# Clustered attention and feed-forward: one-hot rows by a wide transposition and small DMAs, a finer start, squares moved, and GpSimd held during the norm

## The chip, the cores and the metric

The kernel runs on one core of one Trainium2 chip. The metric is device microseconds (us) of the slowest core, here the only one, as the median of several executions. Before the change it took 359.23 us in three runs (358.73 to 359.6). Engines: PE is TensorE, PEld its weight loads, DVE VectorE, ACT ScalarE, POOL GpSimd, SP SyncE, which issues most of the DMAs.

## The reference

```python
# 4 batches, 8 heads, 768 tokens, head size 64, 16 clusters
q_assign = argmax(q_n @ c_n)          # cluster of each query, likewise of each key
mask     = q_assign == k_assign       # attend only inside a cluster
attn     = softmax(where(mask, q @ k.T / 8, -1e9))
x        = attn @ v                   # 3072 tokens x 512
xn       = x / sqrt(mean(x*x) + 1e-6) * rms_g
out      = (silu(xn @ w_gate) * (xn @ w_val)) @ w_out     # 512 -> 1536 -> 512
```

## The kernel before

The work is cut into eight units of half a batch (384 queries by 768 keys, eight heads each). The mask costs no operation of its own: 16 one-hot rows of the cluster stand below the 64 rows of queries and keys, and one product over 80 rows gives the scaled score plus the agreement of the clusters. For each head of a unit ScalarE takes three exponentials of 128x768; "gap n" is the place in TensorE's order ahead of the n-th of them. The first batch has no earlier work to hide its preparation in. For it, the one-hot rows are made pair by pair of heads:

```python
    pads = xp.tile([P, H // 2, 2, NB, 32], BF16, tag="gvT", name="pads")

    def pair_clusters(p, ps=None):        # products with the centroids, maximum, compare
        g, h = divmod(2 * p, HG)
        cl = cluster_products(g, [(h, 0), (h + 1, 0), (h, 1), (h + 1, 1)], ps)
        compare(pads[:, p, :, :, :NC]..., cl, largest(cl))

    def under(n, m, e0=0, e1=2):          # one head's rows, transposed straight into place
        nc.vector.transpose((kext if m else qext)[g][D:D + 32, h, e0 * UQ:e1 * UQ],
                            pads[i:i + 32, n // 2, e0:e1]...)
    def pair(p):
        pair_clusters(p)
        for n in (2 * p, 2 * p + 1):
            under(n, 1)
            under(n, 0, 0, 1)
```

The feed-forward weights come in pieces that GpSimd issues between its casts. Piece i is one DMA of 384 KB for the gate and one for the values:

```python
    def load_gv(i):
        c = slice(i * DF // 4, (i + 1) * DF // 4)
        for w, of in ((wg, moe_w_gate), (wv, moe_w_val)):
            nc.gpsimd.dma_start(out=w[:, :, c], in_=of[:, c].rearrange("(c p) f -> p c f", p=P))
```

At the end of a unit come the squares (ScalarE, `L346`), the norm on VectorE from `sm` over thirteen small steps to the normalized `xn`, and then `tx`, TensorE's transposition of `xn`, which opens the feed-forward part.

The softmax here doesn't subtract the row's maximum and nothing guards it: scores larger than these inputs give would overflow.

## Time and profile before

| what, in the profile of the kernel before | us |
|---|---|
| span | 357.5 |
| first exponential | 14.00 |
| exponential 17, the third of head 5 | 34.16 |
| half clock of TensorE | 26.7 to 30.1 |
| norm of unit 0, start of `sm` to start of `xn` | 44.13 to 48.20 |
| `tx` of unit 0 | 49.32 |
| from `tx` to the end | 308.2 |

A row of a timeline has the start, the duration, the engine, the line of the program, the operation, out<-in with the shapes, and in brackets how long the engine stood idle ahead of it and what ended that. Two rows of ScalarE set the pace of the first 50 us:

```profile
14.00 1.69 ACT L312 ACTIVATE pT<-s,off 128x768 bf16<-128x768 f32 x2 [1.33 <-PE s L308]
...
34.16 2.48 ACT L312 ACTIVATE pT<-s,off 128x768 bf16<-128x768 f32 x3 [0.23 <-PE s L308]
```

The list of DMA issues (who issued it, how often, KB of one, median us from issue to landing) has two small transfers that took long:

```profile
gcol<-in_moe_rms_g_dram SPq DMA_DIRECT2D x1, 2.0 KB, 7.6
...
hold<-inv SPq DMA_DIRECT2D x1, 3.0 KB, 5.5
```

### The profile page before, as it was taken

The page shows a single profiled execution, that of the slowest core. Times are in us where ns is not written, and L with a number is a line of the kernel's source. Part 1 is how long each engine was busy: PE and PEld are TensorE (multiplying, and loading weights), DVE is VectorE, ACT ScalarE, POOL GpSimd, SP SyncE. Part 2 cuts the span into 40 slices and gives each one's busy share as a digit, 9 for nine tenths or more (in the row PEclk, how much of TensorE's full clock was granted, in tenths as well). Part 3 has the DMA queues.
Part 4 walks back from the last instruction along what each step waited for, and adds up shares of the span by engine and source line. Part 5 has one row for each costly group of instructions (what it writes and reads, how often), then busy time and mean ns, then how long its engine had stood idle before and what let it go on. Part 6 is the DMA issues. An engine that isn't in the chain of part 4 may idle for free.

```text
span 357.5 us, 7997 instructions
## 1 busy us (share of the span) xinstructions
PE 342.4 (96%) x3031; PEld 209.2 (59%) x3031; DVE 232.7 (65%) x562; ACT 264.4 (74%) x471; POOL 113.6 (32%) x228
## 2 busy tenths in 40 slices
PE   7879889999999999999999999999999999999995
PEld 3546555655675656655576556756566656655552
DVE  4899889886367764686457864687546654675430
ACT  5787987887787878877698877978778877852431
POOL 5899431894042802444042801436000000000000
PEclk9998999999999999999999999999999999999999
DMA  8999999271153112610130001000100001001002
GB/s 275 360 171 139 271 268 296 65 227 47 59 162 106 24 59 83 191 33 16 60 119 2 19 35 59 2 6 21 59 31 0 2 32 59 3 0 62 28 2 89
DMA packets 27158, 31.62 MB, mean 88 GB/s; under 512 B 4464, under 2 KB 24176, under 8 KB 27120
## 3 DMA queue, kind: packets, MB, share of 16 engines
q1 hardware_dynamic: 17808, 24.69, 20.8%
q0 software_dynamic: 8880, 5.91, 10.1%
q8 instruction: 24, 0.39, 0.5%
q10 hardware_dynamic: 432, 0.52, 0.4%
q14 instruction: 14, 0.11, 0.1%
HBM read 28.35 MB, written 6.29 MB: 97 GB/s over the span
## 4 chain that ended last, share of the span: by engine, by line
PE 85%; ACT 7%; DVE 5%; issue 2%; DMA 1%; ACTq 0%; DVEq 0%
PE o L403 17%; PE val L381 16%; PE gate L381 16%; PE s L308 16%; PE acc L326 9%; PE tq L205 5%; ACT pT L312 4%; PE sc L235 3%; PE warm L117 2%; PE tx L368 1%; ACT xn L346 1%; DVE kext L292 1%; DVE mx L243 1%; ACT qkT L211 1%; DMA out_dram<-o_sb 1%
## 5 line engine op out<-in xcount | busy, mean ns | idle before, releaser
L312 ACT ACTIVATE pT<-s,off 128x768 bf16<-128x768 f32 x192 | 171.5, 904 | 37.8 <-PE s L308 37.1
L308 PE MATMUL s<-qext,kext 80*128 80x384 bf16 x384 | 94.6, 328 | 4.3 <-ACT pT L312 3.1
L390 DVE SCALAR_TENSOR_TENSOR th<-th,gate 128x384 f32<-128x384 f32 x84 | 46.3, 552 | 49.7 <-ACT th L389 49.3
L381 PE MATMUL val<-xnT,wv 128*128 128x384 bf16 x384 | 78.1, 326 | 0.6 <-ACT th L387 0.5
L381 PE MATMUL gate<-xnT,wg 128*128 128x384 bf16 x384 | 78.3, 325 | 0.0
L403 PE MATMUL o<-wo,gvT 128*128 128x512 bf16 x288 | 70.4, 378 | 0.4 <-ACT o_sb L414 0.3
L308 PEld LDWEIGHTS <-kext 80*128 80x128 bf16 x384 | 37.3, 99 | 37.5 <-issue 12.0
L220 POOL CAST qext<-qkT 64x384 bf16<-64x384 f32 x64 | 32.4, 510 | 83.7 <-ACT qkT L211 59.4
L389 ACT ACTIVATE th<-gate 128x384 f32<-128x384 f32 x84 | 41.0, 488 | 15.8 <-PE gate L381 15.4
L381 PEld LDWEIGHTS <-wv 128*128 128x128 bf16 x384 | 36.2, 97 | 26.5 <-issue 4.4
L394 DVE SCALAR_TENSOR_TENSOR gvT<-th,val 128x384 bf16<-128x384 f32 x84 | 46.1, 549 | 6.4 <-PE val L381 1.7
L326 PEld LDWEIGHTS <-pT 128*128 128x128 bf16 x1152 | 43.6, 97 | 11.1 <-DVE x L333 1.9
L381 PEld LDWEIGHTS <-wg 128*128 128x128 bf16 x384 | 35.9, 97 | 23.9 <-issue 2.5
L326 PE MATMUL acc<-vbf,pT 128*128 128x65 bf16 x1152 | 45.8, 193 | 2.0 <-DVE x L333 1.6
L403 PEld LDWEIGHTS <-gvT 128*128 128x128 bf16 x288 | 26.9, 97 | 26.2 <-issue 0.5
L276 POOL DMA_DIRECT2D qext<-oh x48 | 23.1, 490 | 37.2 <-DVE oh L265 37.0
L205 PE MATMUL tq<-ident_f,qk 128*128 128x128 f32 x192 | 31.0, 281 | 1.2 <-PE c_ps L179 0.8
L211 ACT ACTIVATE qkT<-tq 128x384 f32<-128x384 f32 x56 | 26.4, 498 | 2.9 <-PE tq L205 2.2
L205 PEld LDWEIGHTS tq<-ident_f,qk 128*128 128x128 f32 x192 | 23.5, 143 | 7.1 <-PE c_ps L179 1.1
L414 ACT COPY o_sb<-o 128x512 f32<-128x512 f32 x23 | 13.5, 585 | 19.1 <-PE o L403 18.6
L369 DVE TENSOR_SCALAR xnT<-tx,gcol 128x384 bf16<-128x384 bf16 x32 | 12.6, 414 | 22.4 <-PE tx L368 22.3
L276 POOL DMA_DIRECT2D kext<-oh x48 | 23.1, 488 | 1.3 <-DMA qext<-oh 1.1
(68 smaller groups left out, 261.0 us busy)
## 6 DMA issues: line engine op xcount, KB each, us to landing
qk<-in_q_dram SPq DMA_DIRECT2D x32, 192.0 KB, 4.1
vs<-in_v_dram SPq DMA_DIRECT2D x32, 192.0 KB, 4.1
out_dram<-o_sb SPq DMA_DIRECT2D x23, 256.0 KB, 2.0
qk<-in_k_dram SPq DMA_DIRECT2D x30, 192.0 KB, 4.2
wg<-in_moe_w_gate_dram POOLq DMA_DIRECT2D x4, 384.0 KB, 6.8
wv<-in_moe_w_val_dram POOLq DMA_DIRECT2D x4, 384.0 KB, 8.9
wo<-in_moe_w_out_dram POOLq DMA_DIRECT2D x3, 512.0 KB, 22.8
qext<-oh POOLq DMA_DIRECT2D x48, 12.0 KB, 1.6
```

The lines of the kernel that those rows point to most:

```text
L205: nc.tensor.transpose(ps[:, i * P:(i + 1) * P], qk[:, part, 2 * i:2 * i + 2].rearrange("p t d -> p (t d)"), ident_f)
L211: nc.scalar.activation(to, ps, ACT.Copy, scale=by)
L220: on.tensor_copy(to, of)
L276: on.dma_start(out=ext[D:D + NC, h, e * UQ:(e + 1) * UQ], in_=put[g, m][32 * h + e * NC:32 * h + (e + 1) * NC])
L308: nc.tensor.matmul(ps[:, j, :w] if nt == HT else flat[:, j * w:(j + 1) * w], lhsT=kext[g % 4][:KR, hh, kc * P:(kc + 1) * P], rhs=qext[g % ...
L312: nc.scalar.activation(pT[u, h][:, n * i:n * i + n, :w], of, ACT.Exp, bias=off, scale=scale * ZS)
L326: nc.tensor.matmul(acc[:, h % 2, t], lhsT=pT[u, h][:, kc, t * P:(t + 1) * P], rhs=vbf[g % 4][:, hh, kc % HT * 2 + kc // HT], start=kc == 0 ...
L381: nc.tensor.matmul(ps, lhsT=w[:, c, f * P:(f + 1) * P], rhs=xnT[u][:, c, :n], start=c == 0, stop=c == CC - 1)
L389: nc.scalar.activation(th, ps, ACT.Tanh, scale=0.5)
L390: nc.vector.scalar_tensor_tensor(th, th, 1.0, ps, op0=ALU.add, op1=ALU.mult)
L394: nc.vector.scalar_tensor_tensor(gvT[u][:, f, :n], gates[u], 0.5, ps, op0=ALU.mult, op1=ALU.mult)
L403: nc.tensor.matmul(outs[u], lhsT=gvT[u][:, f, t * P:(t + 1) * P], rhs=wo[:, f], start=f == 0, stop=f == FC - 1)
```

## The change

Its intent is to take work off VectorE in the first 40 us and off ScalarE at the end of unit 0, so that the first `tx` comes earlier. For head pairs 1 to 3 one wide transposition of 128x768 replaces the four (later two more) narrow ones, and four DMAs carry the rows into place. The room won on VectorE takes key casts from GpSimd and the squares of unit 0 from ScalarE. The first pair's transpositions are split, so that the first score needs less; the centroid transposition gets another buffer; and GpSimd is made to wait during the norm. Cut to its core:

```diff
-        c_ps = ps_g.tile([P, P], F32, tag="gen", name="c_ps")
+        c_ps = ps_s.tile([P, P], F32, tag="s", name="c_ps")
 ...
-    pads = xp.tile([P, H // 2, 2, NB, 32], BF16, tag="gvT", name="pads")
+    both = xp.tile([P, 5, S], BF16, tag="gvT", name="pads")
+    pads = both[:, :2]...;  rows = both[:, 2:]
 ...
     def pair(p):
         pair_clusters(p)
-        for n in (2 * p, 2 * p + 1):
-            under(n, 1)
-            under(n, 0, 0, 1)
+        nc.vector.transpose(rows[:, p - 1], pads[:, 1].rearrange("p e b c -> p (e b c)"))
+        for n in (2 * p, 2 * p + 1):
+            for m in (1, 0):
+                i = 32 * (2 * m + n % 2)
+                nc.sync.dma_start(out=(kext if m else qext)[n // HG][D:D + NC, n % HG], in_=rows[i:i + NC, p - 1])
 ...
-    under(0, 1)
+    under(0, 1, 0, 1)
     under(0, 0, 0, 1)
+    under(0, 1, 1, 2)
 ...                                     # squares of unit 0
+        if u == 0:
+            nc.vector.scalar_tensor_tensor(xn[u][:, t, c], xs[u][:, t, c], 1.0, xs[u][:, t, c], op0=ALU.mult,
+                                           op1=ALU.mult, accum_out=to)
 ...                                     # order of casts and loads
     vcast(0)
+    load_gv(0)
     vcast(1)
 ...                                     # keys of heads 4 to 7 are cast on VectorE
+        casts(dve, 4, K0, K1)
 ...                                     # GpSimd held during the norm of unit 0
-            hooks = {(1, 0, 1): lambda: rms(0)}
+            idle = const.tile([P, 1], BF16)
+            hooks = {(1, 0, 1): lambda: (rms(0), nc.gpsimd.tensor_copy(idle, xn[0][:, HT - 1, DM - 1:]))}
```

More of the change, by code (lines that the diff above doesn't have):

```diff
@@ L277, in place @@
                              in_=put[g, m][32 * h + e * NC:32 * h + (e + 1) * NC])
-    pads = xp.tile([P, H // 2, 2, NB, 32], BF16, tag="gvT", name="pads")
-    nc.gpsimd.memset(pads, 0.0)
+    both = xp.tile([P, 5, S], BF16, tag="gvT", name="pads")
+    pads = both[:, :2].rearrange("p k (e b c) -> p k e b c", e=2, c=32)
+    rows = both[:, 2:]
+    nc.gpsimd.memset(pads[:, 0, :, :, NC:], 0.0)
+    nc.gpsimd.memset(pads[:, 1, :, :, NC:], 0.0)
     def pair_clusters(p, ps=None):
@@ L286, in pair_clusters, with pair @@
         cl = cluster_products(g, [(h, 0), (h + 1, 0), (h, 1), (h + 1, 1)], ps)
-        compare(pads[:, p, :, :, :NC].rearrange("p e b c -> p b e c"), cl, largest(cl))
+        compare(pads[:, min(p, 1), :, :, :NC].rearrange("p e b c -> p b e c"), cl, largest(cl))
     def under(n, m, e0=0, e1=2):
-        g, h = divmod(n, HG)
         i = 32 * (2 * m + n % 2)
-        nc.vector.transpose((kext if m else qext)[g][D:D + 32, h, e0 * UQ:e1 * UQ],
-                            pads[i:i + 32, n // 2, e0:e1].rearrange("p e b c -> p (e b c)"))
+        nc.vector.transpose((kext if m else qext)[0][D:D + 32, n, e0 * UQ:e1 * UQ],
+                            pads[i:i + 32, 0, e0:e1].rearrange("p e b c -> p (e b c)"))
+    def pair(p):
+        pair_clusters(p)
+        nc.vector.transpose(rows[:, p - 1], pads[:, 1].rearrange("p e b c -> p (e b c)"))
[3 more added lines that the diff above has]
+                nc.sync.dma_start(out=(kext if m else qext)[n // HG][D:D + NC, n % HG], in_=rows[i:i + NC, p - 1])
     pT = {}
@@ L345, in squares @@
         c = slice(DM - 2 * D, DM) if last else slice(0, DM - 2 * D)
-        nc.scalar.activation(xn[u][:, t, c], xs[u][:, t, c], ACT.Square, accum_out=sq[u][:, int(last), t:t + 1])
+        to = sq[u][:, int(last), t:t + 1]
+        if u == 0:
+            nc.vector.scalar_tensor_tensor(xn[u][:, t, c], xs[u][:, t, c], 1.0, xs[u][:, t, c], op0=ALU.mult,
+                                           op1=ALU.mult, accum_out=to)
+        else:
+            nc.scalar.activation(xn[u][:, t, c], xs[u][:, t, c], ACT.Square, accum_out=to)
     def rms(u):
@@ L472, in tokens, with casts @@
         trans(g, h, 0, on)
-    def gp_cast(n, *what):
+    def casts(on, n, *what):
         for m, e in what:
-            cast(nc.gpsimd, n // HG, n % HG, m, (e,))
+            cast(on, n // HG, n % HG, m, (e,))
+    K0, K1, Q0, Q1 = (1, 0), (1, 1), (0, 0), (0, 1)
+    pool_, dve = nc.gpsimd, nc.vector
     trans(0, 0, 1)
@@ L484 @@
     pair_clusters(0, ps_s.tile([P, UQ], F32, tag="s", name="sc"))
-    gp_cast(0, (1, 0), (1, 1), (0, 0))
-    cast(nc.scalar, 0, 1, 1)
-    gp_cast(1, (0, 0))
+    casts(pool_, 0, K0, Q0, K1)
+    casts(pool_, 1, K0, Q0)
     load_v(0)
@@ L495 @@
     tokens(0, 2)
-    gp_cast(2, (1, 0), (1, 1), (0, 0))
-    gp_cast(0, (0, 1))
-    gp_cast(1, (0, 1))
+    casts(pool_, 2, K0, K1, Q0)
     tokens(0, 3)
-    gp_cast(3, (1, 0), (1, 1), (0, 0))
     tokens(1, 0)
+    casts(pool_, 3, K0, K1, Q0)
+    casts(nc.scalar, 1, K1)
     busy(2)
-    under(0, 1)
+    under(0, 1, 0, 1)
     under(0, 0, 0, 1)
+    under(0, 1, 1, 2)
     under(1, 1)
     under(1, 0, 0, 1)
+    casts(pool_, 0, Q1)
+    casts(pool_, 1, Q1)
     vcast(0)
+    load_gv(0)
     vcast(1)
@@ L520, in second_batch @@
             load_v(n)
-    def pair(p):
-        pair_clusters(p)
-        for n in (2 * p, 2 * p + 1):
-            under(n, 1)
-            under(n, 0, 0, 1)
     def gap1():
@@ L530, in gap1, with gap8 @@
         tokens(1, 1)
-        load_gv(0)
-        gp_cast(2, (0, 1))
-        gp_cast(3, (0, 1))
+        casts(pool_, 2, Q1)
+        casts(pool_, 3, Q1)
         vcast(2)
         vcast(3)
-        gp_cast(4, (1, 0), (1, 1), (0, 0))
-        for n in range(H, H + HG):
-            load_qk(n)
-        nc.sync.dma_start(out=gcol, in_=moe_rms_g.rearrange("(c p) -> p c", p=P), allow_slow_non_contiguous=True)
+        load_qk(H)
+        load_qk(H + 1)
     def gap5():
         pair(2)
-        gp_cast(5, (1, 0), (1, 1), (0, 0))
+        load_qk(H + 2)
+        load_qk(H + 3)
+        casts(dve, 4, K0, K1)
+        casts(pool_, 4, Q0)
+        casts(pool_, 5, Q0)
+        load_gv(1)
         vcast(4)
         vcast(5)
-        load_gv(1)
-        gp_cast(6, (1, 0), (1, 1), (0, 0))
-        gp_cast(7, (1, 0), (1, 1), (0, 0))
+    def gap8():
+        pair(3)
+        nc.sync.dma_start(out=gcol, in_=moe_rms_g.rearrange("(c p) -> p c", p=P), allow_slow_non_contiguous=True)
+        for n in (5, 6, 7):
+            casts(dve, n, K0, K1)
+        for n in (6, 7):
+            casts(pool_, n, Q0)
+        load_gv(2)
         vcast(6)
@@ L551, in gap5, with gap12 @@
         for n in (4, 5):
-            gp_cast(n, (0, 1))
-        for i in range(2, 4):
-            load_gv(i)
+            casts(pool_, n, Q1)
+        load_gv(3)
         for n in (6, 7):
-            gp_cast(n, (0, 1))
+            casts(pool_, n, Q1)
         for c in range(0, FC, 4):
             load_o(c)
+    def gap12():
+        under(0, 0, 1, 2)
+        under(1, 0, 1, 2)
+        more()
     early = [lambda h=h, m=m: trans(1, h, m) for h in (2, 3) for m in (1, 0)]
-    late = [lambda h=h, m=m: (under(h, 0, 1, 2) if m else under(h + HG, 0, 1, 2), trans(2, h, m, nc.vector))
-            for h in range(HG) for m in (1, 0)]
-    first = {1: gap1, 2: early[0], 3: early[1], 4: lambda: (early[2](), early[3]()), 5: gap5, 8: lambda: pair(3),
+    late = [lambda h=h, m=m: trans(2, h, m, nc.vector) for h in range(HG) for m in (1, 0)]
+    first = {1: gap1, 2: early[0], 3: early[1], 4: lambda: (early[2](), early[3]()), 5: gap5, 8: gap8, 12: gap12,
              14: lambda: (more(), second_batch())}
```

## The prediction

> **What bounds the kernel now.** I read the page's slices first (where is TensorE not full?), then the chain, then each engine's timeline from 5 to 52 us.
>
> ```profile
> PE   7879889999999999999999999999999999999995
> ...
> DVE  4899889886367764686457864687546654675430
> ...
> PEclk9998999999999999999999999999999999999999
> ```
>
> A digit is 8.94 us. From the seventh on TensorE is full: what comes after about 60 us can only move as a block. Anything won is won before the feed-forward part of unit 0 begins, with its first transposition `tx` at 49.32 us. Before that, VectorE is the full engine, and one slice of TensorE runs at a lower clock. Stretches of 2 us (columns: TensorE, weight loads, VectorE, ScalarE, GpSimd busy; granted clock; DMA share; GB/s):
>
> ```profile
> 24.00:26.00 2.00, 0.74 (x5) 0.20 (x2) 1.92 (x4) 1.69 (x2) 2.00 (x4) 1.00 0.26 28
> 26.00:28.00 2.00, 1.69 (x21) 1.13 (x22) 1.93 (x4) 0.00 (x0) 1.82 (x5) 0.68 0.99 149
> 28.00:30.00 2.00, 2.00 (x7) 0.87 (x6) 1.94 (x4) 1.48 (x2) 1.88 (x5) 0.50 1.31 203
> ```
>
> The timelines say what TensorE and ScalarE stood for (brackets: idle time before, and its releaser):
>
> ```profile
> 26.31 0.88 PE L326 MATMUL acc<-vbf,pT 128*128 128x65 bf16 x18 [1.56 <-DVE x L333]
> ...
> 24.86 0.57 DVE L292 STREAM_TRANSPOSE qext<-pads 32x384 bf16<-32x384 bf16 x1
> ...
> 25.69 0.56 DVE L333 TENSOR_TENSOR x<-acc,inv 128x384 f32<-128x384 f32 x1
> ...
> 28.30 0.90 ACT L312 ACTIVATE pT<-s,off 128x768 bf16<-128x768 f32 x1 [2.31 <-PE s L308]
> ```
>
> Attention output `x` of the first two heads queued behind pair 2's four one-hot transpositions; TensorE stood 1.56 us for the accumulator; its clock then fell to 0.5; ScalarE stood 2.31 us. The second limit comes at the end of unit 0, from 38 to 48 us. The chain of work there (start, duration):
>
> ```profile
> 38.56 0.50 ACT xn L346 x2
> ...
> 39.85 0.50 ACT xn L346 x2
> ...
> 41.02 0.62 ACT xn L346 x2
> ...
> 43.40 0.42 ACT xn L346 x3
> ...
> 48.45 0.48 PE s L308 x2
> ```
>
> ScalarE is full (10.00 of 10 us from 40 to 50), and the squares L346 lie in its row of exponentials. Beside it runs the norm on VectorE, almost as late:
>
> ```profile
> 44.13 0.21 DVE L353 TENSOR_TENSOR sm<-ss 128x3 f32<-128x3 f32 x1 [1.07 <-ACT xn L346]
> ...
> 44.58 0.36 DVE L124 TENSOR_SCALAR half<-ms 128x3 int32<-128x3 int32 x1
> 44.97 0.41 DVE L126 TENSOR_SCALAR yi<-half 128x3 int32<-128x3 int32 x1
> ...
> 48.20 1.28 DVE L358 TENSOR_SCALAR xn<-x,ny 128x512 bf16<-128x512 f32 x3
> ...
> 86.12 0.17 DVE L124 TENSOR_SCALAR half<-ms 128x3 int32<-128x3 int32 x1
> 86.32 0.17 DVE L126 TENSOR_SCALAR yi<-half 128x3 int32<-128x3 int32 x1
> ```
>
> The same chain from `sm` to `xn` takes 4.07 us here and 2.57 us in unit 1 (85.72 to 88.29), where GpSimd does nothing; in unit 0 GpSimd casts at that time.
>
> **What the Trainium skill says.** "SBUF — State Buffer", Who interferes with whom: VectorE and GpSimd share a port pair, held by one of them for a whole instruction; copies, casts and scalar operations in a two-port mode and operations with two SBUF inputs contend with GpSimd. The 0.17 against 0.36 to 0.41 us above agrees. "VectorE: DVE Perf Modes", The three transpose paths: the transposition works in independent 32x32 blocks; so a wide one should cost by its length only, and the trace agrees: 128x384 bf16 (L265) took 576 ns, 32x384 (L292) 570. "DMA: Bandwidth & Descriptors", Queues, rings and completion order: each ring is consumed in order, and an engine alternates between the rows that have work. The trace shows both ends: 12 KB one-hot copies land in 1.6 us when little else moves, while the 3 KB `hold` took 5.5 us amid weight loads. "TensorE: Matmul & The Clock Gate", What's actually happening: an idle window of about 3.4 us halves the clock; the half-clock stretch here lasted from about 26.6 to 30.0.
>
> **The change part by part.** I count a gap for each of unit 0's 24 exponentials (0 to 23; 0.79 us apart on ScalarE when nothing holds it).
>
> *Start.* TensorE's third transposition starts at 7.25 us; the one of the centroids ended at 6.44, and their copies on VectorE at 7.14. I take it that the buffer of `c_ps` held it; with `c_ps` elsewhere about 0.8 us falls away (the trace names only the centroid product as releaser). The first pair in halves: 0.57 instead of 0.97 us before the first score, 0.4 us. First exponential: 14.00 - 1.2 = 12.8 us.
>
> *VectorE.* Removed for pairs 1 to 3: six transpositions of 0.97 and twelve of 0.57 = 12.7 us. Added: three wide ones of 0.97 = 2.9; eight casts of keys, 0.36 each (48 such casts in the trace average 356 ns) = 2.9; squares, three of about 0.56 and three of about 0.3 = 2.6; the extra half of the first pair 0.2. Net about 4 us less, and in another order. Walking it: pair 0 takes 0.58 + 0.56 + 0.66 + 3x0.57 + 0.97 + 0.57 and gaps = 5.2 us from 8.9, so to 14.1. Pair 1 (0.6 + 0.6 + 0.65 + 0.97 = 2.8) to 16.9. Pair 2's products come after score 5, about 18.7: to 21.6, casts of head 4 to 22.4, `x` of the first heads to 23.2 (25.69 + 0.56 = 26.25 before). So the stall of 1.56 us and the clock drop at 26 us go. But then the queue gets long: pair 3, 2.8 to 26.0; six casts, 2.2 alone; two late halves for queries, 1.2; only then `x` of heads 2 and 3 (0.8): 30.2 if nobody contends. GpSimd casts at the same time; if half its 0.5 us cast is waited for at each of the eight casts, 2 us more: 32. I take 31.2. Before, that `x` ended at 32.0. TensorE needs it for head 4 in gap 16, and ScalarE can be there by about 28 to 29.5. So the old stall comes back later, smaller in effect: exponential 17 starts at about 32.8 instead of 34.16. Gain so far 1.4 us, of which part may be lost to a new clock drop.
>
> *One-hot rows by DMA.* The wide result ends at 16.9; SyncE issues one row block in about 0.4 us, key then query, and landing takes about 2 us: head 2 at about 19.8. Exponential 6 could start at 12.8 + 6x0.79 + six copies of 0.37 + 0.2 = 19.95, its score 0.5 earlier: a wait of some 0.4 us. Pair 2: from 21.6, behind the loads of heads 8 and 9 in the same ring, 24.5 to 25.5, against a wish of about 24.4. Pair 3: about 29, against 32. These waits lie before the VectorE queue of gap 16 and are hidden by it unless they exceed 2 us.
>
> *Squares.* ScalarE loses three of 0.50 and three of 0.30 (pace of instruction and accumulator read in the chain): 2.4 us of a stretch in which it is full. VectorE gets them after eight single transpositions of queries (8x0.60) have left it, so it has room. All 2.4 counted.
>
> *Norm.* 4.07 to 2.57 = 1.5 us, needed so that VectorE keeps up: with exponential 23 ending near 38.8, `x` of the last heads is done at 40.5, squares 41.3, norm 43.9, `xn` 45.2. ScalarE and TensorE reach the same point at 38.8 + 6x0.79 + four copies of 0.38 = 45.1, with `tx` just after. So both paths end about together, at 45.2 to 45.4; the norm's gain isn't added a second time.
>
> *Sum.* `tx` at 49.32 - 1.4 - 2.4 = 45.5; the walk gives 45.3. About 4 us. After it TensorE is full, but GpSimd's casts of the next batch (4x1.58 = 6.3 us) now follow the norm instead of ending before it; TensorE idled about 1.7 us between 49.8 and 66, and I let that grow by a few tenths of a us. Memory traffic is denser too. Net 3.9 us: 359.2 - 3.9 = about 355.3.
>
> **Rivals.** First, the rows come late: each one-hot copy queues among weights and token loads, and one lands after 5 us as `hold` did. Then head 2 waits about 3 us, head 4 about as long, TensorE idles and drops its clock, and some 3 us of the gain go: 358. For it: DMA share around 1.0 from 2 to 24 us. Against: before those rows SyncE's ring should be empty, because the loads of heads 8 to 11 now come behind them, and a block is only 16 packets. Second, VectorE's queue in gap 16 is worse than I think: contention makes the casts 0.8 us each, and the clock halves for 3.4 us while TensorE has score, transposition and product in each gap (0.9 us a gap at full clock before): 357. For it: VectorE 9.1 to 9.6 of 10 us all through; against: the order was presumably chosen by trying. Third, casts don't contend, exponentials run nearly at ScalarE's own pace, and `tx` comes at 42 to 43: 352 to 352.5. Fourth, the gain is real at 45 us but the part after it waits for casts, one-hot copies or weights that did not move: 357.
>
> **Range and chances.** The walk ends at 355.3; first and second rival lie 2 to 3 us above, the third 3 us below. Eight in ten: 352.4 to 357.6. Faster by over 2% means below 352.0, that is, 7.2 us; ScalarE's own minimum gives at most about 7. So 0.06. Slower by over 2% needs a wait of 11 us that nothing suggests: 0.01. Within 2%: 0.93.
>
> **What would show it.** First exponential near 12.8; exponential 6 with a wait below 1 us, its releaser a product waiting for a DMA; no clock drop at 26 us, but TensorE waiting for `x` (L333) near 29 to 31; no L346 on ScalarE in unit 0; 13 norm steps of 0.16 to 0.17; `tx` at about 45.3; the rest moved as a block. I am wrong if the row copies take over 4 us to land, if VectorE's casts average over 0.6 us, if the third transposition still starts at 7.25, or if TensorE idles over 3 us between 50 and 66 us of the old count.

## The result, and the profile after

The changed kernel took 359.62 us (four runs, 359.34 to 359.93); the kernel before, in the same rounds, 359.09 (358.73 to 359.6). The ratio is 1.0014, with an interval of 0.9996 to 1.0031: the same. The class "same" had 0.93 in the prediction, but the time lies above its range, 2.0 us over 357.6.

| us in the profile | before | after | predicted |
|---|---|---|---|
| span | 357.5 | 357.4 | |
| first exponential | 14.00 | 12.55 | 12.8 |
| landing of a one-hot block | none | 5.3 (keys), 5.5 (queries) | about 2 |
| TensorE's wait ahead of head 2 | none | 4.31 | 0.4 |
| exponential 6 | 21.18 | 24.05 | 19.95 + 0.4 |
| half clock | 26.7 to 30.1 | 23.1 to 26.5 | none at 26 |
| exponential 17 | 34.16 | 36.34 | 32.8 |
| `sm` to `xn`, start to start | 4.07 | 2.57 | 2.57 |
| `tx` | 49.32 | 49.47 | 45.3 |
| from `tx` to the end | 308.2 | 307.9 | as a block |

The page's slices first, for TensorE and its clock:

```profile
PE   8958989999999999999999999999999999999996
...
PEclk9989999999999999999999999999999999999999
```

The first two digits of TensorE rose by one each, and the third fell from 7 to 5; the lower clock is still there, now in the third slice instead of the fourth. The loss begins in that slice, 17.9 to 26.8 us. The timeline of TensorE names it:

```profile
23.21 0.80 PE L319 MATMUL s<-qext,kext 80*128 80x384 bf16 x2 [4.31 <-DMA qext<-pads]
...
34.90 0.72 PE L337 MATMUL acc<-vbf,pT 128*128 128x65 bf16 x18 [1.13 <-DVE x L344]
...
49.47 0.67 PE L384 MATMUL tx<-ident,xn 128*128 128x128 bf16 x9
```

The score of head 2 waited 4.31 us for its one-hot query rows. ScalarE shows the won start, and the hole:

```profile
12.55 1.69 ACT L323 ACTIVATE pT<-s,off 128x768 bf16<-128x768 f32 x2 [0.47 <-PE s L319]
...
24.05 0.90 ACT L323 ACTIVATE pT<-s,off 128x768 bf16<-128x768 f32 x1 [4.13 <-PE s L319]
```

In the chain of work that ended last, the transfer itself is now a link (start, duration, engine, what):

```profile
15.97 0.99 DVE pads L300
16.98 0.60 SPq L304
17.62 5.45 DMA qext<-pads
23.21 0.80 PE s L319 x2
```

VectorE was on time: the wide transposition ended at 16.96, where the prediction had 16.9. SyncE issued the four blocks at 16.98, 17.62, 18.25 and 18.89. Nothing was late before the transfers were handed over; the time went between issue and landing:

```profile
kext<-pads SPq DMA_DIRECT2D x6, 24.0 KB, 5.3
qext<-pads SPq DMA_DIRECT2D x6, 24.0 KB, 5.5
```

What did the DMA engines do then? The rows of GpSimd show what had been queued just before (the issue's start and its duration):

```profile
14.58 0.90 POOL L191 DMA_DIRECT2D wg<-in_moe_w_gate_dram  x1
15.47 0.76 POOL L191 DMA_DIRECT2D wv<-in_moe_w_val_dram  x1
```

And the queues, first in the window from 20 to 21 us, then from 21 to 22 (packets, MB, share of 16 engines; q0 is GpSimd's queue with the weights, q1 the one with SyncE's transfers):

```profile
q0 software_dynamic: 258, 0.19, 125.2%
...
q1 hardware_dynamic: 5, 0.01, 2.4%
```

```profile
q1 hardware_dynamic: 149, 0.14, 62.7%
q0 software_dynamic: 42, 0.03, 19.7%
```

All four blocks had been handed over by 19.5, and still from 20 to 21 us the engines took 258 packets of weights, about 16 on each of 16 engines, and 5 of everything on q1. At 20.94 the first block packet runs, and then q1 has the engines. In the packet records I counted what went between the end of the first block's issue and its first packet, shared out over 16 engines (the records don't name the engine): 55 packets of weights each, or 60 from the start of that issue. The other pairs' blocks took as long (5.5 to 6.4 us for pair 2, 4.8 to 6.1 for pair 3), behind token loads in SyncE's own queue too, but TensorE did not stand for them.

The price of the wait is more than the wait, because the clock of TensorE halves after it (columns: TensorE, weight loads, VectorE, ScalarE, GpSimd busy; granted clock; DMA share; GB/s):

```profile
20.00:22.00 2.00, 0.00 (x0) 0.00 (x0) 1.93 (x4) 0.00 (x0) 2.00 (x4) 1.00 1.08 189
22.00:24.00 2.00, 0.79 (x3) 0.43 (x4) 0.85 (x2) 0.00 (x0) 2.00 (x5) 0.76 1.02 220
24.00:26.00 2.00, 2.00 (x23) 1.42 (x21) 0.00 (x0) 1.79 (x2) 1.94 (x4) 0.50 1.22 218
```

In the last line TensorE is busy all of the 2 us at a clock of 0.50, while VectorE has nothing to do. It had run ahead, and then stood 3.24 us for the product of heads 0 and 1:

```profile
26.11 0.20 DVE L342 RECIPROCAL inv<-acc 128x6 f32<-128x6 f32 x1 [3.24 <-PE acc L337]
...
34.28 0.56 DVE L344 TENSOR_TENSOR x<-acc,inv 128x384 f32<-128x384 f32 x1
...
45.37 0.16 DVE L369 TENSOR_TENSOR sm<-ss 128x3 f32<-128x3 f32 x1
...
45.77 0.17 DVE L124 TENSOR_SCALAR half<-ms 128x3 int32<-128x3 int32 x1
...
47.94 1.28 DVE L374 TENSOR_SCALAR xn<-x,ny 128x512 bf16<-128x512 f32 x3
```

So its long queue began late, and `x` of heads 2 and 3 was done at 34.28 + 0.56 = 34.84 instead of the predicted 31.2. That gives TensorE the second wait, 1.13 us at 34.90. From `sm` on, the norm goes as predicted: 2.57 us to `xn`, its small steps 0.16 to 0.17.

From exponential 17 to `tx` the kernel before took 49.32 - 34.16 = 15.2 us, the kernel after 49.47 - 36.34 = 13.1. So 2 us were won there, and 1.45 at the start; the stretch between them gave them back.

### The profile page after: what moved, and what is told of

Its sections match the earlier page's. It is cut to its first block, busy times and chain, and to the rows that moved or that the text cites. A ratio compares the mean times of both kernels' runs of the same rounds, so it can differ in the third digit from the quotient of the medians.

```text
span 357.4 us, 8008 instructions
## 1 busy us (share of the span) xinstructions
PE 342.0 (96%) x3031; PEld 209.1 (58%) x3031; DVE 226.7 (63%) x568; ACT 261.7 (73%) x458; POOL 107.9 (30%) x223
## 4 chain that ended last, share of the span: by engine, by line
PE 83%; DVE 8%; ACT 4%; DMA 2%; issue 1%; SPq 0%; ACTq 0%; DVEq 0%
PE o L419 17%; PE val L397 16%; PE gate L397 16%; PE s L319 15%; PE acc L337 9%; PE tq L205 5%; PE sc L235 3%; ACT pT L323 2%; DMA qext<-pads 2%; DVE kext L220 1%; PE tx L384 1%; PE warm L117 1%; DVE scT L238 1%; DVE mx L243 1%; DVE qext L295 1%
## 5 line engine op out<-in xcount | busy, mean ns | idle before, releaser
L397 PEld LDWEIGHTS <-wv 128*128 128x128 bf16 x384 | 36.2, 97 | 26.8 <-issue 4.8
L419 PEld LDWEIGHTS <-gvT 128*128 128x128 bf16 x288 | 26.8, 97 | 26.3 <-issue 0.5
L276 POOL DMA_DIRECT2D qext<-oh x48 | 23.1, 490 | 29.7 <-DVE oh L265 29.7
L211 ACT ACTIVATE qkT<-tq 128x384 f32<-128x384 f32 x56 | 26.5, 498 | 3.4 <-PE tq L205 2.7
```

The costliest lines, as they stand in the source:

```text
L211: nc.scalar.activation(to, ps, ACT.Copy, scale=by)
L276: on.dma_start(out=ext[D:D + NC, h, e * UQ:(e + 1) * UQ], in_=put[g, m][32 * h + e * NC:32 * h + (e + 1) * NC])
L397: nc.tensor.matmul(ps, lhsT=w[:, c, f * P:(f + 1) * P], rhs=xnT[u][:, c, :n], start=c == 0, stop=c == CC - 1)
L419: nc.tensor.matmul(outs[u], lhsT=gvT[u][:, f, t * P:(t + 1) * P], rhs=wo[:, f], start=f == 0, stop=f == FC - 1)
```

## The experiments

Fourteen kernels ran. All of them compute the reference's result correctly. Theory Q (queue): a block must wait until each DMA engine has worked off weight packets queued before it, and this wait and its half clock eat the gain. The first expectation calls it "backlog", and sets against it that a block costs 5 us by itself ("intrinsic"). Rival V: VectorE's longer queue is what holds the kernel, and would hold it with prompt blocks too. Rival F: the later casts and one-hot copies of the next batch eat the gain after `tx`. Further points are what the squares, the start and the hold are worth by themselves.

### Weights after the blocks

```diff
-    load_gv(0)          # and load_gv(1), (2), (3) at their places in gaps 5 and 8
 ...                     # in gap 8, GpSimd first waits for the last block:
+        nc.gpsimd.tensor_copy(landed[D:D + 1], qext[1][D:D + 1, 3, :1])
+        for i in range(4):
+            load_gv(i)
         for c in range(0, FC, 4):
             load_o(c)
```

> The changed kernel, but GpSimd issues all weight loads only after the last one-hot block of pair 2 has landed. Theory backlog (the blocks of pair 1 wait because the DMA engines first work off the two weight loads already queued): a block lands in 2 to 2.5 us instead of 5.3, TensorE's wait of 4.31 us before head 2 falls below 1 us, no half clock at 23 us, and the time falls by 2 to 4 us. Theory intrinsic (a block of 16 partitions from SyncE costs 5 us by itself): landing stays at 5 us, the wait stays at about 4 us, the time stays within 0.5 us. Theory VectorE: the wait goes, but the wait for x in gap 16 grows by as much, and the time stays within 1 us.

One correction to that text: the edit holds the weights until the last block of pair 3 has landed, not that of pair 2. Measured: 362.35 us (360.68 to 364.95), ratio 1.0095 (1.0032 to 1.0159). The time got worse, but the stage in question did what Theory Q says. Landing:

```profile
kext<-pads SPq DMA_DIRECT2D x6, 24.0 KB, 2.8
qext<-pads SPq DMA_DIRECT2D x6, 24.0 KB, 2.5
```

Pair 1's blocks landed in 2.2 us in the mean (2.5 for head 2, 1.9 for head 3), so a block does not cost 5 us by itself. On TensorE:

```profile
20.55 0.48 PE L319 MATMUL s<-qext,kext 80*128 80x384 bf16 x2 [1.53 <-DMA qext<-pads]
...
45.46 0.67 PE L384 MATMUL tx<-ident,xn 128*128 128x128 bf16 x9
...
76.39 0.82 PE L319 MATMUL s<-qext,kext 80*128 80x384 bf16 x4 [3.66 <-DMA kext<-oh]
```

The wait fell from 4.31 to 1.53 us (not below 1, as expected), there is no half clock near it, and `tx` comes at 45.46, the predicted place (45.3). Rival V falls by this: the same VectorE work, with prompt blocks, lets `tx` come 4.0 us earlier than in the changed kernel. But from `tx` to the end it took 314.0 us instead of 307.9, 6.1 more, and the third line shows part of it. GpSimd shows why:

```profile
61.95 0.49 POOL L276 DMA_DIRECT2D qext<-oh  x1 [2.24 <-DMA wg<-in_moe_w_gate_dram]
...
65.94 0.49 POOL L276 DMA_DIRECT2D qext<-oh  x1 [3.51 <-DMA wv<-in_moe_w_val_dram]
```

The one-hot copies of the next batch go out by the same GpSimd queue, and their issues stood behind the late weights, one after the other. TensorE then waited 3.66 us and ran at half clock from 77.9 to 81.3. So the weights must be out of the way at both ends.

### Weights in two steps

```diff
-    load_gv(0)
 ...                     # end of gap 5: after pair 1's last block has landed
+        nc.gpsimd.tensor_copy(landed[D:D + 1], qext[0][D:D + 1, 3, :1])
+        load_gv(0)
 ...                     # gap 8: after pair 2's last block has landed
+        nc.gpsimd.tensor_copy(landed2[D:D + 1], qext[1][D:D + 1, 1, :1])
+        for i in range(1, 4):
+            load_gv(i)
         for c in range(0, FC, 4):
             load_o(c)
```

> The changed kernel with the first weight piece issued only when pair 1's last one-hot block has landed, the other three and the output weights when pair 2's have (in e1 everything waited for pair 3's last block, not pair 2's as its expectation said; it won 4 us before tx and lost 6 after it to one-hot copies standing behind weights). Theory backlog: blocks of pairs 1 and 2 land in 2 to 3 us, tx comes at 45 to 46 us; the weights are over about 5 us sooner than in e1, so the later loss shrinks from 6 to 0 to 3 us: 356 to 359. If the later loss came from something else than the end of the weights, it stays at 6 us and the time at 362.

Measured: 357.0 us in five runs (356.61 to 357.33), ratio 0.9934 (0.9922 to 0.9947). This is the best kernel, 0.66% faster than the one before and faster than the changed one. Its TensorE rows:

```profile
20.10 0.48 PE L319 MATMUL s<-qext,kext 80*128 80x384 bf16 x2 [1.87 <-DMA qext<-pads]
...
46.58 0.67 PE L384 MATMUL tx<-ident,xn 128*128 128x128 bf16 x9
```

Pair 1's blocks landed in 2.4 us in the mean (2.8 for head 2), the wait is 1.87, `tx` comes 2.9 us earlier than in the changed kernel, and from there to the end it takes 307.9 us, exactly as there. Rival F falls by this: the part after `tx` moved as a block. Two things still stand in the way of 355.3: the wait of 1.87 us and a stretch of half clock from 21.7 to 25.1. Half clock came after waits of 1.56 us (the kernel before) and 1.87 us (here), and not after 1.53 us (the first experiment); what decides it was not tested. The expectation missed twice: `tx` was to come at 45 to 46, and pair 2's blocks, expected in 2 to 3 us, took 3.4 to 6.8, again beside weights and behind token loads. A caution: 0.67 us of the 2.9 are already there at the first exponential (11.88 against 12.55), where the two kernels do not differ yet; TensorE's first six transpositions took 0.82 us in this one profile against 1.38. The five timed runs don't depend on that profile.

### How many weights: none, half, one piece, two

Two edits change only what is queued ahead of pair 1's blocks. The first doubles it (almost: the last of its four DMAs is issued together with the first block), the second halves it.

```diff
     vcast(0)
     load_gv(0)
+    load_gv(1)          # and taken away in gap 5
     vcast(1)
```

> The changed kernel with two weight pieces instead of one queued ahead of pair 1's blocks. The first piece's packets took the engines from about 16 to 21 us. Theory backlog: the blocks start only when the second piece is done too, about 5 us later: landing of pair 1's blocks 9 to 10.5 us, TensorE's wait before head 2 about 9 us. If engines alternate between queues, landing stays at 5 to 6 us.

```diff
     vcast(0)
-    load_gv(0)
+    load_gv(0, slice(0, 1))      # gate half alone; the value half goes with load_gv(1)
     vcast(1)
```

> The changed kernel with half a piece (gate weights alone) queued ahead of pair 1's blocks, the other half issued with the second piece. Theory backlog: landing of pair 1's blocks about 3 us, wait before head 2 about 1.5 us instead of 4.3, half clock perhaps still; 357 to 359. If engines alternate, landing stays near 5 us.

Doubled: 360.5 us (one look, state unknown). Halved: 358.8, ratio 0.9986 (0.9962 to 1.001); here TensorE stood a second time, 2.30 us ahead of head 4 for pair 2's rows. TensorE's wait ahead of head 2, doubled and then halved:

```profile
24.02 0.54 PE L319 MATMUL s<-qext,kext 80*128 80x384 bf16 x2 [4.50 <-DMA qext<-pads]
```

```profile
21.20 0.48 PE L319 MATMUL s<-qext,kext 80*128 80x384 bf16 x2 [2.70 <-DMA qext<-pads]
```

| weights queued ahead of pair 1's blocks | landing, mean of keys / of queries, us | weight packets per engine between the end of the first block's issue and its first packet | wait, us |
|---|---|---|---|
| none (first two experiments) | 2.2 to 2.4 | 0 | 1.53, 1.87 |
| half a piece | 3.8 / 4.6 | 22 | 2.70 |
| one piece (the change) | 5.3 / 5.0 | 55 | 4.31 |
| two pieces | 5.5 / 5.4 | 63 | 4.50 |

From none to one piece the landing grows with what is queued. From one to two it hardly grows. Theory Q in its plain form, in which everything queued ahead is worked off first, would have added as much again; it falls. What fits is a bounded wait: a block that comes to an empty queue lets up to some 60 packets per engine go first, and no more. At the 16 packets per us seen above, the 55 of the changed kernel are 3.4 us, an estimate; the 5.3 us measured is the unloaded 2.2 plus 3.1.

It would be tempting to conclude that an engine serves the weights' queue in turns of that length. The same profile says no. Later, when both queues of the changed kernel have work all the time (26 to 28 us), the engines took nearly as many packets from one as from the other:

```profile
q0 software_dynamic: 275, 0.21, 66.9%
q1 hardware_dynamic: 254, 0.33, 54.7%
```

By the spacing of the packet records they alternate one by one there: a weight packet follows the one before it on its engine after 132 ns, with one of q1 between, where it took 60 ns from 18 to 20.8 us. What differs for pair 1 is that SyncE's queue was empty when the block came. Why a block then waits for so many packets stays open.

### Weight DMAs in small pieces

If the wait ends with the DMA that is running, smaller DMAs should shorten it. Piece 0 is issued as eight DMAs of one row chunk each, which is 8 packets on an engine; the second kernel does the same with piece 1.

```diff
         for w, of in ((wg, moe_w_gate), (wv, moe_w_val)):
-            nc.gpsimd.dma_start(out=w[:, :, c], in_=of[:, c]...)
+            for k in range(CC):              # for i == 0; the second kernel: for i in (0, 1)
+                nc.gpsimd.dma_start(out=w[:, k:k + 1, c], in_=of[k * P:(k + 1) * P, c]...)
```

> The changed kernel with the first weight piece issued as eight DMAs of one row chunk (8 packets an engine) instead of two of four chunks (32 packets an engine). If an engine turns after the DMA it has begun, pair 1's blocks land in about 3 us, TensorE's wait before head 2 falls to about 1.5 to 2 us, and the time to about 357 to 358. If it takes some 64 packets whatever the DMAs, landing stays at 5 us or above and the time at 359.5 or above, as GpSimd issues longer.

> As e13, the second piece split as well. Same reading for pair 2's blocks (5 to 6 us in the changed kernel): about 3 us if engines turn at the end of a DMA, unchanged if not. GpSimd's six more issues of about 0.5 to 0.75 us may delay casts and cost up to 2 us.

Measured: 360.63 us, ratio 1.0037 (1.0015 to 1.006), and 359.2, ratio 1.0026 (0.9979 to 1.0073). An engine now took 12 to 16 packets of weights before a block's first, not 55, and pair 1's landing fell to 4.3 (keys) and 3.5 to 3.7 (queries). TensorE's wait ahead of head 2 fell from 4.31 to 2.92 and 2.78 us, in the direction that smaller DMAs should give. But much of the fall has another cause: eight issues take longer, so only five of them, 40 packets an engine, had been issued when the first block's issue ended, and 22 of these were still to be taken, against 57 in the changed kernel. With 25 to be taken, the half piece let 22 go first. So the size of the DMAs is shown to matter by some 6 to 10 packets, and no more. Pair 2's blocks in the second kernel (3.8 to 4.6 us) are no test, since its second piece was issued after them. The split did not pay: GpSimd needs 4.4 us to issue eight DMAs instead of 1.66 for two, its casts come later, and TensorE's wait for `x` at about 34 us grew from 1.13 to 2.73 (1.80 in the second). The four blocks of the first kernel still came apart, between 18.2 and 21.2 us, and one of SyncE's own issues took 1.66 us instead of 0.6.

### The blocks on another queue

```diff
-                nc.sync.dma_start(out=...[D:D + NC, n % HG], in_=rows[i:i + NC, p - 1])
+                nc.scalar.dma_start(...)    # pair 1 in gap 4, pair 2 in gap 10, pair 3 in gap 12
```

> The changed kernel with the one-hot blocks issued from ScalarE's queue (its own ring, in which nothing else stands) instead of SyncE's. If the wait is in SyncE's ring, blocks land in about 2 us. Theory backlog (the engines are shared): still about 4 to 6 us. Theory intrinsic: about 5 us. The time itself is of no use here, as ScalarE pays 12 issues of about 0.6 us.

Measured: 365.73 us (one look, state unknown). The median landing of all six barely changed:

```profile
kext<-pads ACTq DMA_DIRECT2D x6, 24.0 KB, 4.8
qext<-pads ACTq DMA_DIRECT2D x6, 24.0 KB, 4.7
```

Pair 1's own blocks took 5.5 to 6.5 us. So it is no congestion of SyncE's ring: a block in a third ring, with nothing else in it then, waits as long. Between the end of the first block's issue and its first packet (16.97 to 20.76 us) each engine took 32 packets of weights and 18 of SyncE's loads. The rest of the loss is the issues in ScalarE's row and their later place, which this experiment does not separate.

### Pair 1 without DMA

```diff
     def pair(p):
         pair_clusters(p)
+        if p == 1:
+            for n in (2, 3):
+                under(n, 1)
+                under(n, 0, 0, 1)
+            return
 ...                     # the wide transposition and the DMAs for pairs 2 and 3 only; in gap 12:
-        under(1, 0, 1, 2)
+        for n in (1, 2, 3):
+            under(n, 0, 1, 2)
```

> The changed kernel, but pair 1 gets its one-hot rows by direct VectorE transpositions as before; pairs 2 and 3 by DMA. Theory backlog: no wait before head 2; head 4 (pair 2) now waits for its blocks, about 2 to 3 us, since they too stand behind weights; the time falls by 1 to 3 us. Theory intrinsic: the same for pair 1, and pair 2's landing stays at 5 us. Theory VectorE: the 2 to 3 us of transpositions put back appear as a longer wait for x in gap 16 and the time stays within 1 us of the changed kernel.

Measured: 359.37 us, ratio 0.9996 (0.9963 to 1.0028). The wait ahead of head 2 is gone, and it comes back one pair later, behind piece 1 of the weights:

```profile
28.16 0.80 PE L325 MATMUL s<-qext,kext 80*128 80x384 bf16 x2 [2.13 <-DMA qext<-pads]
```

The same with the later weights held as in the two-step kernel, and piece 0 at the changed kernel's place:

```diff
-        load_gv(1)              # in gap 5, and load_gv(2), load_gv(3) in gap 8
 ...                             # gap 8: after pair 2's last block has landed
+        nc.gpsimd.tensor_copy(landed[D:D + 1], qext[1][D:D + 1, 1, :1])
+        for i in range(1, 4):
+            load_gv(i)
```

> A version meant to beat e5: pair 1's rows by direct transposition (as e2), the first weight piece where the changed kernel has it, the other weights only when pair 2's last block has landed (as e5). If backlog is the whole cause, pair 2's blocks land in 2 to 3 us, no wait before head 2, none over 0.5 us before head 4, tx at 45 to 46 us and 355.5 to 357. If VectorE's 2.1 us more of transpositions count, the wait for x (1.31 us in e2) stays and the time is 357 to 358.5.

Measured: 359.84 us (358.42 to 361.78), ratio 1.0022 (0.9995 to 1.005). Pair 2's blocks, with no weights left in the queue, landed in 1.9 us. With both DMA waits mended, VectorE's queue is what holds it:

```profile
32.58 0.78 PE L343 MATMUL acc<-vbf,pT 128*128 128x65 bf16 x18 [3.10 <-DVE x L350]
```

Four narrow transpositions cost 0.97 + 0.57 + 0.97 + 0.57 = 3.1 us where the wide one costs 1.0, and the late halves of heads 2 and 3, which the wide one covered, cost another 2 x 0.57, so VectorE has 3.2 us more ahead of that `x`. Here the wait of the prediction's second rival is real, though from more work and not from contention. `tx` came at 48.77, not at the 45 to 46 expected. The DMAs are therefore not a mistake; their company is.

### The parts by themselves

The start alone, on the kernel before:

```diff
-        c_ps = ps_g.tile([P, P], F32, tag="gen", name="c_ps")
+        c_ps = ps_s.tile([P, P], F32, tag="s", name="c_ps")
 ...
-    gp_cast(0, (1, 0), (1, 1), (0, 0))
+    gp_cast(0, (1, 0), (0, 0), (1, 1))
 ...
-    under(0, 1)
+    under(0, 1, 0, 1)
     under(0, 0, 0, 1)
+    under(0, 1, 1, 2)
```

> The kernel before with only the start changed (c_ps elsewhere, first pair in halves). First exponential at 12.6 to 12.8 instead of 14.0 us. If VectorE's row after it passes the gain on, 0.8 to 1.2 us are won in the time; if a load (v, tokens) sets what follows, nothing.

Measured: 357.96 us, ratio 0.9957 (0.9941 to 0.9972); first exponential at 12.45. It is worth 1.3 us by the times, and the prediction had 1.2.

The squares of unit 0 on VectorE, on the kernel before:

```diff
+        if u == 0:
+            nc.vector.scalar_tensor_tensor(xn[u][:, t, c], ..., op0=ALU.mult, op1=ALU.mult, accum_out=to)
+        else:
             nc.scalar.activation(xn[u][:, t, c], xs[u][:, t, c], ACT.Square, accum_out=to)
```

> The kernel before with only the squares of unit 0 moved to VectorE. If ScalarE's full row from 38 to 48 us sets the time, as the prediction counted, 2 us or more are won. If VectorE, which is at 95 percent there, sets it, 0 to 1 us are won or something is lost, because its queue gets 2.6 us longer ahead of the norm.

Measured: 361.65 us, ratio 1.0062 (1.0032 to 1.0093): a loss of 2.2 us. Beside GpSimd's casts three of the six squares took longer than in the changed kernel (`xn<-x` 128x384 is 0.55 in the changed kernel, 128x128 is 0.28 to 0.29):

```profile
42.82 0.84 DVE L348 SCALAR_TENSOR_TENSOR xn<-x 128x384 bf16<-128x384 f32 x1
...
45.18 0.63 DVE L348 SCALAR_TENSOR_TENSOR xn<-x 128x128 bf16<-128x128 f32 x1
```

(The expectation's "95 percent" is off: VectorE was busy for 8.2 us of the 10 from 38 to 48.) The norm began later, and TensorE stood for it:

```profile
49.84 2.28 PE L373 MATMUL tx<-ident,xn 128*128 128x128 bf16 x12 [1.96 <-DVE xn L363]
```

With the hold of GpSimd added to that kernel:

```diff
-            hooks = {(1, 0, 1): lambda: rms(0)}
+            idle = const.tile([P, 1], BF16)
+            hooks = {(1, 0, 1): lambda: (rms(0), nc.gpsimd.tensor_copy(idle, xn[0][:, HT - 1, DM - 1:]))}
```

> The kernel before with squares on VectorE and GpSimd held during the norm (e3 had the squares alone and lost 2.2 us: squares of 0.55 and 0.29 us took up to 0.84 and 0.63 with GpSimd casting, the norm came out at 50.6 and TensorE's clock halved). If the contention with GpSimd was the cause, the loss goes and 0 to 2 us are won against the kernel before. If VectorE's longer queue was it, the loss stays above 1 us.

Measured: 359.66 us, ratio 1.0013 (0.9995 to 1.003); `sm` to `xn` is 2.56 us again, and the squares are back at 0.55 to 0.56 and 0.28 to 0.29. The hold gives those 2 us back, and no more.

From the other side, the changed kernel with the squares back on ScalarE, and the changed kernel without the hold:

```diff
-        if u == 0:
+        if u < 0:
```

> The changed kernel with the squares of unit 0 back on ScalarE. The prediction counted 2.4 us for them: then 361.5 to 362. If the norm on VectorE or the clock sets tx here, less than 1 us is lost.

```diff
-            hooks = {(1, 0, 1): lambda: (rms(0), nc.gpsimd.tensor_copy(idle, ...))}
+            hooks = {(1, 0, 1): lambda: rms(0)}
```

> The changed kernel without holding GpSimd during the norm. The prediction put 1.5 us on the hold but as one of two paths that end together. In e3 against e7 the hold was worth 2.0 us. Expected 360.5 to 362; if ScalarE's row alone sets tx in the changed kernel, no change (359.6).

Squares on ScalarE: 361.1 us, ratio 1.005 (1.0036 to 1.0064), so by the medians, which come from different rounds, the move is worth 361.1 - 359.6 = 1.5 us in the changed kernel. The profiles show it more directly: from exponential 17 to `tx` it takes 15.17 us with the squares back on ScalarE, as in the kernel before, and 13.13 without, so 2.0 us. Without the hold: 359.44, ratio 1.0002 (0.9985 to 1.0019), not to be told from the changed kernel. In its profile the values scaled to `xn` took 1.97 us instead of 1.28, and `tx` came at 49.83 instead of 49.47; but its first exponential came 0.35 us later too, and from exponential 17 to `tx` it took the same 13.13 us.

## Why the prediction was right or wrong

**What bounds it: right.** Only what happens ahead of `tx` counts. From `tx` to the end it took 308.2, 307.9 and, in the two-step kernel, 307.9 us. The fourth rival, a loss after `tx`, came neither in the changed kernel nor in that one; the kernel that held the weights too long made it.

**Start: right.** 1.2 us predicted, 1.3 measured alone (357.96), and the first exponential at 12.55 for a predicted 12.8.

**VectorE's walk to pair 1: right.** The wide result was to end at 16.9 and ended at 16.96.

**One-hot rows: this is the step that failed.** "SyncE issues one row block in about 0.4 us, key then query, and landing takes about 2 us: head 2 at about 19.8 [...] a wait of some 0.4 us." Landing took 5.3 and 5.5 us and the wait was 4.31. The 2 us came from copies that land in 1.6 us "when little else moves", and little else moves only later in the kernel; the `hold` row, 5.5 us, was the one that applied. With no weights queued the blocks land in 2.2 us, so the figure was nearly right for another surrounding; but the blocks that head 2 waits for then took 2.5 to 2.8 us, and TensorE still stood 1.53 to 1.87 us, not 0.4. The issue was off as well, in a small way: 0.59 us a block, not 0.4.

**The argument that dismissed the first rival** was "SyncE's ring should be empty [...] and a block is only 16 packets". The ring was empty, and an empty ring didn't help: on a queue of its own a block of pair 1 took 5.5 to 6.5 us. What counts is what the other queues hold. The section of the Trainium skill that the prediction named (DMA: Bandwidth & Descriptors, Queues, rings and completion order) has a sentence that bears on it: an engine "drains a whole packet (≈9-17 descriptors typical, spec ceiling ≤64) from one row's ring before switching". The prediction took from it only that engines alternate, and from 26 to 28 us they do. The 55 and 63 packets counted here (60 and 67 from the start of the issue) lie near that ceiling, not near the typical figure, if a packet record of the trace is one of the page's descriptors, which no run here decides. That such a turn is what the block waited for is not shown, since the same engines alternate one by one later.

**"These waits [...] are hidden by it unless they exceed 2 us."** The wait exceeded it, and it could not have been hidden, because the queue of gap 16 is fed by TensorE: VectorE stood 3.24 us for the products of heads 0 and 1, and all that follows moved with it. The queue itself was as long as foreseen: from the end of the first `x` to the end of the second, 23.2 to 31.2 in the prediction, 26.90 to 34.84 in the profile, 8.0 and 7.9 us. That agreement is luck in part: the prediction had allowed 1 us for contention with GpSimd, and the six casts in it took 2.3 us, 0.1 more than without; but for 0.83 us VectorE stood for pair 3's centroid product, which was not foreseen. The half clock that the first rival named came too, for 3.4 us. The prediction's page names an idle window of about 3.4 us for it; after 3.41 us without any TensorE work that is what came here, but in the kernel before and in the two-step kernel TensorE was busy for 1.84 and 1.57 us of the 3.41 ahead of it, so a wait well short of the window was enough. That rival put the time at 358 and was nearest; the wait for `x` that the second one feared (1.13 us) came in its wake, not from contention.

**Squares: mechanism right, size off.** "All 2.4 counted"; 1.5 by the times and 2.0 in the profiles, measured by putting them back. And the kernel before shows that the move loses 2.2 us where GpSimd casts at the same time, so it depends on the other parts, as the prediction said of VectorE's room.

**Norm: right, but worth nothing here.** 2.57 us and steps of 0.16 to 0.17 as predicted; without the hold the time is the same within 0.3%. The prediction had not added it a second time.

**Sum.** Gains of 1.45 us at the start and about 2 from exponential 17 on stand against a loss in between. With prompt blocks `tx` comes at 45.46, which is the predicted 45.3: the rest of the walk holds, if with two errors against each other (exponential 17 at 32.33 instead of 32.8, and 13.1 us from there to `tx` instead of 12.5). One reading was wrong without weight: TensorE idled 1.0 us between 49.8 and 66, not 1.7. That the time follows is shown only in part. The kernel with `tx` at 45.46 paid later for its late weights, and the best kernel, at 357.0, still has a wait of 1.87 us and a half clock. Whether 355.3 can be reached was not shown.

## What to carry to other kernels

A small transfer that TensorE waits for must be kept clear of large loads that are queued on the same DMA engines, whatever queue it is in. Look for another small transfer in the same stretch of the profile and take its landing time, not the one of a quiet stretch. Loads moved out of its way must still be done before the next user of their queue needs it: holding the weights for too long cost 6 us after `tx`, holding them in two steps won 2.6 us over the changed kernel. An engine's saved work on the critical path is worth its measured microseconds only if what feeds that engine isn't late.

## What the Trainium skill lacked or had wrong

- DMA: Bandwidth & Descriptors, Queues, rings and completion order: it gives 9 to 17 descriptors as typical before an engine switches rings. Neither case here is like that. A block that came to an empty ring waited for 55 (one piece of weights) and 63 (two pieces) weight packets per engine; with both rings busy, the engines alternated packet by packet (275 of weights and 254 of SyncE's in 2 us). The page has no figure for what the first case costs a small transfer: a 24 KB block took 2.2 us with nothing queued, 3.8 to 4.6 behind half a piece, 5.0 to 5.3 behind a piece and 5.4 to 5.5 behind two.
- SBUF — State Buffer, Who interferes with whom: it names who contends, and the trace agrees, but it has no figure for this pair. A square with its sum took up to 0.84 instead of 0.55 us (128x384) and up to 0.63 instead of 0.28 (128x128) beside GpSimd's casts.
- On none of the pages that I read: what GpSimd pays to issue a load. Here it was 1.66 us for a weight piece in two DMAs, and 4.4 us in eight.
